# Causal attention and a gated feed-forward on one core: the last two batches' feed-forward as one product of 2 x 2 blocks

## Chip, cores, metric

One core of one Trainium2 chip runs the kernel. The metric is the device time of one execution in microseconds.

## What is computed

Four batches of 12 heads, 448 positions and 64 values a head go through causal attention; the result, 768 features for each of 1792 tokens, goes through a gated feed-forward of width 1536. All in float32.

```python
scores = scale * np.matmul(q, k.transpose(0, 1, 3, 2))
scores = np.where(mask, -1000000000.0, scores)
...
attn = attn / (np.sum(attn, axis=-1, keepdims=True) + 1e-09)
return np.matmul(attn, v).astype(np.float32)
...
gate = 1.0 / (1.0 + np.exp(-(x @ w_gate)))
val = x @ w_val
return (gate * val @ w_out).astype(np.float32)
```

## The kernel before

**Units.** The feed-forward of one batch is a unit (`unit_items`). Its first layer has 12 row blocks of the width (`KF`), each once for the gate and once for the value, with 6 K tiles (`KD`): 144 steps. The second has 6 row blocks of the output with 12 K tiles: 72 steps. A step is a triple: float32 is made of a high half (fp32r, 'xh', 'wh', 'gh') and a low one ('xl', 'wl', 'gl'), and three matmuls of 128x128 by 128x448 (L582) give high x high, high x low and low x high. One weight block serves 6 steps. Its halves are cut by ScalarE (L564) and by L566, which runs on VectorE in unit 0 and on POOL (GpSimd) afterwards. In unit 0 the weights come as int64 words, which ScalarE and VectorE (L549 to L556) turn into float32 that is also stored to DRAM ('wdram'); the later units load them from there (L561).

**First layer's end.** ScalarE takes the tanh out of PSUM (L603), VectorE multiplies (L609), ScalarE and POOL cut the product into halves (L611, L612). A unit's output leaves through ScalarE (L627).

**Attention.** Heads go in pairs, 6 pairs a batch. Batches 0 and 1 use blocks of 112 and TensorE transposes. Batches 2 and 3 (`WIDE`) use blocks of 128: scores in two bursts (L385), softmax on VectorE and ScalarE (L400, L406, L414), scaling on POOL (L421), 32x32 transposes on VectorE into 'room' (L438, L441), and then 16 transfers a pair (L447), each 32 partitions by 512 columns, which move the 32x32 blocks to the partitions where the product with V (L464, `wpv`) wants them. The product of a pair follows its last scores by two pairs. Its features are cut into halves by L351 and L352.

**Order.** Nothing is issued as it is written. Each piece is given to `Plan.op` with an engine, a cost and, for TensorE, a due time; `Plan.order` takes one piece after another, on each engine the ready one that is due first, and the program is emitted in that order. The main loop sets the due times: attention of batch 0 first, then unit `u` with the attention of batch `u + 1` spread over it; unit 3 has none beside it. Each engine runs its own list in order.

[...]

## Time and profile before

| | us |
|---|---|
| median of 3 runs | 692.42 (690.48 to 693.71) |
| the profiled execution | 692.2 |
| its span | 690.5 |
| PE busy, PEld busy | 677.6, 572.3 |
| DVE, ACT, POOL busy | 314.1, 335.3, 366.7 |
| HBM read, written | 88.08 MB, 19.66 MB |

PE is TensorE, PEld its weight loads, DVE VectorE, ACT ScalarE. Busy times of different engines overlap, so none of them is a share of the end time by itself: what an engine's time is worth shows in the stage where it runs.

### The profile page before, as it was taken

To read this page: it belongs to the slowest core of one execution; us is meant where nothing else is said; L and a number is where in the kernel's file an instruction comes from. 1 tells how busy PE (TensorE), PEld (TensorE's weight loads), DVE (VectorE), ACT (ScalarE), POOL (GpSimd) and SP (SyncE) were. 2 spreads that over 40 slices of the span, in tenths; PEclk is the share of its full clock that TensorE was granted. 3 is DMA by queue.
4 is the path that set the end of the run, shared out by engine and by line. 5 is a ranking of instruction groups with operands and counts; after the bars stand their busy time and mean duration, and the time that the engine had idled before them with its cause. 6 is when DMAs were issued, how large, how long until landed. Compare 5 with 4: busy or idle time off the path is not lost.

```text
span 690.5 us, 11031 instructions
## 1 busy us (share of the span) xinstructions
PE 677.6 (98%) x3888; PEld 572.3 (83%) x3888; DVE 314.1 (45%) x820; ACT 335.3 (49%) x721; POOL 366.7 (53%) x352
## 2 busy tenths in 40 slices
PE   7989999999999999999999999999999999999997
PEld 4546887888888888888889888888889999999997
DVE  4898998897897244353520044345440001001000
ACT  6774677667665444545532354455432333333321
POOL 3551551333631367767564467765764456666642
PEclk9999999999999999999999999999999999999999
DMA  5564686687787545545575445544645333333331
GB/s 201 188 223 158 237 304 243 204 292 252 245 298 288 169 153 155 167 142 174 162 227 176 134 133 170 174 126 140 187 140 178 124 127 115 100 106 115 116 130 41
DMA packets 45559, 121.06 MB, mean 175 GB/s; under 512 B 7104, under 2 KB 10176, under 8 KB 45504
## 3 DMA queue, kind: packets, MB, share of 16 engines
q1 hardware_dynamic: 45504, 120.35, 53.6%
q8 instruction: 31, 0.51, 0.3%
q14 instruction: 24, 0.20, 0.1%
HBM read 88.08 MB, written 19.66 MB: 156 GB/s over the span
## 4 chain that ended last, share of the span: by engine, by line
PE 94%; DVE 2%; POOL 1%; DMA 1%; ACT 1%; issue 0%; SPq 0%; ACTq 0%
PE m L582 77%; PE m L464 3%; PE s L270 3%; PE s L385 3%; PE m L343 3%; PE t L319 3%; POOL sm L306 1%; PE t L385 1%; DVE sm L283 1%; DMA room<-in_wp_dram 1%; DVE pt L330 1%; DMA raw<-in_qkt_dram 0%; ACT sm L287 0%; DVE xl L352 0%; ACT wd L549 0%
## 5 line engine op out<-in xcount | busy, mean ns | idle before, releaser
L566 POOL TENSOR_TENSOR wl<-wr,wh 128x768 fp32r<-128x768 f32 x108 | 199.1, 1843 | 167.7 <-ACT wh L564 160.8
L582 PE MATMUL m<-xh,wh 128*128 128x448 f32 x576 | 214.9, 373 | 0.0
L564 ACT CAST wh<-wr 128x768 fp32r<-128x768 f32 x144 | 120.2, 835 | 194.6 <-PE m L582 92.0
L582 PE MATMUL m<-xh,wl 128*128 128x448 f32 x576 | 210.8, 366 | 0.0
L582 PE MATMUL m<-xl,wh 128*128 128x448 f32 x576 | 210.7, 366 | 0.0
L582 PEld LDWEIGHTS m<-xh,wh 128*128 128x128 f32 x576 | 108.3, 188 | 24.0 <-issue 14.0
L582 PEld LDWEIGHTS m<-xh,wl 128*128 128x128 f32 x576 | 108.2, 188 | 8.8
L582 PEld LDWEIGHTS m<-xl,wh 128*128 128x128 f32 x576 | 108.4, 188 | 8.1
L306 POOL TENSOR_SCALAR sm<-sm,r 112x112 f32<-112x112 f32 (+1 forms) x92 | 67.8, 756 | 74.8 <-DVE r L295 56.1
L582 PE MATMUL m<-gh,wh 128*128 128x448 f32 x288 | 106.6, 370 | 0.0
L582 PE MATMUL m<-gl,wh 128*128 128x448 f32 x288 | 105.3, 366 | 0.0
L582 PE MATMUL m<-gh,wl 128*128 128x448 f32 x288 | 105.3, 366 | 0.0
L609 DVE SCALAR_TENSOR_TENSOR gt<-gt,m 128x448 f32<-128x448 f32 x48 | 29.7, 619 | 132.6 <-PE m L582 108.9
L612 POOL TENSOR_TENSOR gl<-gt,gh 128x448 fp32r<-128x448 f32 x48 | 58.2, 1212 | 48.0 <-ACT gh L611 37.2
L406 ACT ACTIVATE sm<-sm,mn 128x128 f32<-128x128 f32 (+3 forms) x84 | 43.9, 524 | 45.2 <-DVE mn L400 45.2
L582 PEld LDWEIGHTS m<-gh,wh 128*128 128x128 f32 x288 | 54.1, 188 | 6.0 <-issue 1.4
L287 ACT ACTIVATE sm<-sm,mn 112x112 f32<-112x112 f32 (+3 forms) x96 | 49.9, 521 | 18.0 <-DVE mn L283 17.7
L582 PEld LDWEIGHTS m<-gh,wl 128*128 128x128 f32 x288 | 54.1, 188 | 4.3
L582 PEld LDWEIGHTS m<-gl,wh 128*128 128x128 f32 x288 | 54.2, 188 | 4.1
L438 DVE STREAM_TRANSPOSE room<-sm 128x384 f32<-128x384 f32 (+2 forms) x84 | 35.4, 447 | 39.7 <-POOL sm L421 35.8
L400 DVE CUSTOM_DVE_ANT_0 sm<-s,mask 128x128 f32<-128x128 f32 (+1 forms) x72 | 29.3, 441 | 47.1 <-PE s L385 46.7
L421 POOL TENSOR_SCALAR sm<-sm,r 128x256 f32<-128x256 f32 (+3 forms) x84 | 41.1, 505 | 7.5 <-DVE r L416 5.7
(46 smaller groups left out, 668.8 us busy)
## 6 DMA issues: line engine op xcount, KB each, us to landing
wr<-wdram SPq DMA_DIRECT2D x108, 384.0 KB, 3.0
room<-in_wp_dram SPq DMA_DIRECT2D x36, 768.0 KB, 5.9
wdram<-wr SPq DMA_DIRECT2D x36, 384.0 KB, 5.2
pt<-room SPq DMA_DIRECT2D x192, 64.0 KB, 2.3
raw<-in_qkt_dram SPq DMA_DIRECT2D x24, 448.0 KB, 4.3
vr<-in_vt_dram SPq DMA_DIRECT2D x24, 256.0 KB, 3.5
out_dram<-gt SPq DMA_DIRECT2D x24, 224.0 KB, 2.0
```

The lines of the kernel that those rows point to most:

```text
L287: plan.op("ACT", act(ne, 0, 2), lambda z=z, sm=sm, i=i, ne=ne, off=off: nc.scalar.activation(out=sm.t[:QB, off:off + ne], in_=sm.t[:QB, of ...
L306: plan.op("PL", 0.27 + w / 1200, lambda args=args: nc.gpsimd.tensor_scalar(**args()), [(r_,)], [(sm, a)])
L385: nc.tensor.matmul(out=sp[z].t[place(z, i), o:o + ne], lhsT=r.t[h, s0:s0 + rows(i)], rhs=r.t[h, S:S + ne])
L400: plan.op("DVE", dve(ne) + 0.16, lambda z=z, y=y, sm=sm, i=i, o=o, ne=ne, off=off, s0=s0, at=at: nc.vector.tensor_tensor_reduce(out=sm.t[a ...
L406: plan.op("ACT", act(ne, 0, 2), lambda z=z, sm=sm, i=i, ne=ne, off=off: nc.scalar.activation(out=sm.t[:, off:off + ne], in_=sm.t[:, off:of ...
L421: plan.op("PL", 0.27 + w / 1200, lambda sm=sm, i=i, o=o, w=w, z=z: nc.gpsimd.tensor_scalar(out=sm.t[:, o:o + w], in0=sm.t[:, o:o + w], sca ...
L438: plan.op("DVE", dve(128 * c) + 0.1, lambda sm=sm, i=i, o=o, c=c, at=at: nc.vector.transpose(out=tv()[:, :, at:at + 32 * c].rearrange("p r ...
L564: plan.op("ACT", act(768), lambda: nc.scalar.copy(hi_.t, t.t), [(t,)], [(hi_,)])
L566: plan.op(eng, cost, lambda: at.tensor_tensor(out=lo_.t, in0=t.t, in1=hi_.t.bitcast(F32), op=ALU.subtract), [(t,), (hi_,)], [(lo_,)], lock ...
L582: nc.tensor.matmul(out=ps.t[:, :S], lhsT=a.t[:, k, :], rhs=b.t if isinstance(b, Buf) else b(), start=(first and z == 0), stop=(last and z ...
L609: plan.op("DVE", dve(S), lambda: nc.vector.scalar_tensor_tensor(out=gg.t, in0=sg.t, scalar=1.0, in1=ps.t[:, :S], op0=ALU.add, op1=ALU.mult ...
L612: plan.op("PL", 1.15, lambda: nc.gpsimd.tensor_tensor(out=gl.t[:, jj], in0=gg.t, in1=gh.t.bitcast(F32), op=ALU.subtract), [(gg,), (gh,)], ...
```

## The change

Units 2 and 3 are replaced by one pair (`pair_items`), which multiplies by Strassen's scheme in the form with seven products. The blocks: the K range in halves (`KH` = 3 tiles), the row blocks in halves, and batch 2 against batch 3. Seven half-size products, named 1 to 7, take the place of eight.

- **Inputs** (`pair_inputs`): features of batches 2 and 3 stay whole in float32 (no L352); VectorE forms the sums, and 21 tiles are cut into halves.
- **Weights** (`in_weights`, `mix`, `cut_half`): for each of 12 pairs of row blocks three loads, four sums of 384 columns on VectorE, and seven cuts of 384 columns by ScalarE and POOL. For the second layer `out_sums` forms sums once and stores them; 21 blocks are cut by ScalarE and VectorE (`cut(..., vector=True)`).
- **Products in PSUM** (`f_in`, `f_out`): 1 and 2 share a bank, 6, 7 and 4 another, 5 and 3 a third. A product adds onto what the bank holds, after VectorE (`plus`) or ScalarE (`scaled`) has read it. The order is a string, `words`: the steady word is 5, 6, 1, 7, 2, 4, 3, where 1 and 2 belong to a block three further on (`AHEAD`).
- **Second layer's inputs** (`out_inputs`): VectorE forms sums, for products 6 and 7 into PSUM ('t'), and cuts most low halves, POOL ten.
- **Attention of batch 3** moves forward: batch 1 is spread over the first 0.95 of unit 0 (`TURN`), batches 2 and 3, twelve pairs, from there to 0.85 of unit 1 (`SPREAD`). In the new order 42 matmuls of the unit (in places 39) stand between two bursts of probability times V, where 36 + 39 stood.
- **Transposed blocks** (`shift`): in place of 16 transfers one write of 1 MB to DRAM and four reads of 256 KB.
- The planner's costs of ScalarE, of the masked reduction and of a triple are changed, and with them the order everywhere.

```diff
+KH = KD // 2
...
+PAIR = 2
+TURN, SPREAD = 0.95, 0.85
+ORDER = "1256743"
+AHEAD = 3
...
-    act = lambda n, psum=0, acc=0: n / 1200 + (0.05 if psum else 0.093) + 0.093 * acc
+    act = lambda n, psum=0, acc=0: n / 1200 + (0.16 if psum else 0.19) + 0.14 * acc
...
+        if b >= PAIR:
+            x = new(f"xh{k}" if b == PAIR else f"xl{k}", [128, S], F32, 2)
+            plan.op("ACT", act(S, 1), lambda: nc.scalar.copy(x.t, vp.t[:, :S]), [(vp,)], [(x,)])
+            xs[b, k] = x
+            return
...
-        for a in range(4):
-            for r in range(4):
-                plan.op("SP", 0.64, lambda a=a, r=r: nc.sync.dma_start(
-                    out=pt.t[32 * r:32 * r + 32, a * WC:a * WC + WC], in_=tv()[32 * a:32 * a + 32, r]),
-                    [(tb, "zero", "end", *[(z, i) for z in range(2) for i in range(3)], (0, 3))], [(pt, (a, r))], extra=2.0)
+        pd = new("pd", [128, 4 * WC], F32, 2, bass.MemoryType.DRAM)
+        plan.op("SP", dma(128 * 4 * WC * 4), lambda: nc.sync.dma_start(out=pd.t, in_=tb.t),
+                [(tb, "zero", "end", *[(z, i) for z in range(2) for i in range(3)], (0, 3))], [(pd,)], extra=2.0)
+        for r in range(4):
+            plan.op("SP", dma(32 * 4 * WC * 4), lambda r=r: nc.sync.dma_start(
+                out=pt.t[32 * r:32 * r + 32, :4 * WC].rearrange("p (a n) -> p a n", a=4),
+                in_=pd.t.rearrange("(a p) (r n) -> r p a n", a=4, r=4)[r]), [(pd,)], [(pt, r)], extra=2.0)
...
+    def add(out, a, b, op, lock=True):
+        plan.op("DVE", dve(S) + 0.08, lambda: nc.vector.tensor_tensor(out=out.at, in0=a.at, in1=b.at, op=op),
+                [a.ref, b.ref], [out.ref], lock=lock)
...
+    def halves(x, hi, lo, pool=False, bank=False):
+
+        plan.op("ACT", act(S, bank), lambda: nc.scalar.copy(hi.at, x.at), [x.ref], [hi.ref])
+        if pool:
+            plan.op("PL", 1.16, lambda: nc.gpsimd.tensor_tensor(
+                out=lo.at, in0=x.at, in1=hi.at.bitcast(F32), op=ALU.subtract), [x.ref, hi.ref], [lo.ref])
+            return
+        plan.op("DVE", dve(S) + 0.08, lambda: nc.vector.tensor_tensor(
+            out=lo.at, in0=x.at, in1=hi.at.bitcast(F32), op=ALU.subtract), [x.ref, hi.ref], [lo.ref], lock=not bank)
...
+            b11, b21, b12, b22 = xa[i], xa[KH + i], xb[i], xb[KH + i]
+            for p in "56743":
+                T[p, i] = rest[p][2 * i:2 * i + 2]
+            halves(b22, *T["3", i])
+            add(b11, b12, b11, ALU.subtract)
+            add(b12, b22, b12, ALU.subtract)
+            add(b22, b22, b11, ALU.subtract)
+            add(b21, b21, b22, ALU.subtract)
+            for p, x in ("5", b11), ("6", b22), ("7", b12), ("4", b21):
+                halves(x, *T[p, i])
...
+        def take():
+
+            ring.append(part(KD * 128, len(ring) % 6))
+            return ring[-1]
...
+        def cut_half(src, at):
+
+            n = st["cuts"] = st.get("cuts", -1) + 1
+            if n % 2 == 0:
+                st["wb"] = [new(tag, [128, KD, 128], F32R, BUFS["ws"]) for tag in ("wh", "wl")]
+            (hi_, lo_), e, w = st["wb"], n % 2, KD * 64
+            f = lambda t: t.rearrange("p k m -> p (k m)")[:, e * w:e * w + w]
+            x = lambda: src.t[:, at * w:at * w + w]
+            plan.op("ACT", act(w), lambda: nc.scalar.copy(f(hi_.t), x()), [(src, at)], [(hi_, e)])
+            plan.op("PL", 1.0, lambda: nc.gpsimd.tensor_tensor(
+                out=f(lo_.t), in0=x(), in1=f(hi_.t).bitcast(F32), op=ALU.subtract), [(src, at), (hi_, e)], [(lo_, e)])
+            return (hi_, lo_), e
...
+        def in_weights(n):
+            j, gv = n // 2, n % 2
+            a = fetch(wdram[2 * j + gv])
+            c = fetch(wdram[2 * (KD + j) + gv])
+            b = take()
+            mix((b, 1, 1), (a, 0, 1), (c, 0, 1), ALU.subtract)
+            mix((c, 0, 1), (c, 0, 1), (c, 1, 1), ALU.add)
+            mix((b, 0, 1), (c, 0, 1), (a, 0, 1), ALU.subtract)
+            mix((a, 1, 1), (a, 1, 1), (b, 0, 1), ALU.subtract)
+            st["from", n] = {"5": (c, 0), "4": (c, 1), "6": (b, 0), "7": (b, 1), "3": (a, 1)}
...
+        def out_sums(m):
+
+            at = lambda mm, half: wdram[2 * KF + 2 * mm + half]
+            a11, a12, a21, a22 = (fetch(at(mm, half), new(tag, [128, KD * 128], F32, BUFS[tag]))
+                                  for mm, half, tag in ((m, 0, "wr"), (m, 1, "wr"), (KH + m, 0, "wr"), (KH + m, 1, "wd")))
+            e = lambda x: (x, 0, 2)
+            mix(e(a22), e(a21), e(a22), ALU.add)
+            mix(e(a21), e(a11), e(a21), ALU.subtract)
+            mix(e(a11), e(a22), e(a11), ALU.subtract)
+            mix(e(a12), e(a12), e(a11), ALU.subtract)
...
+        def plus(out, ps, x, scale):
+
+            b = bank(ps)
+            if scale == 1.0:
+                add(out, b, x, ALU.add, lock=False)
...
+        def f_in(n, p, k, due):
+            st["now"] = due
+            j, gv = n // 2, n % 2
+            if k == 0:
+                if p == "1":
+                    if n == 0:
+                        stage()
+                    st["raw", n] = fetch(wdram[2 * j + gv])
+                if ("from", n) not in st and p in "56":
+                    in_weights(n)
+                if p in "156":
+                    b, tag, bufs = {"1": ("x", "t", 2), "5": ("z", "s", 3), "6": ("y", "m", 3)}[p]
+                    st[b, n] = new(tag, [128, 512], F32, bufs, PSUM)
+                st["w"] = cut_half(*((st["raw", n], "12".index(p)) if p in "12" else st["from", n][p]))
+            ps = st[{"1": "x", "2": "x", "5": "z", "6": "y", "7": "y", "4": "y", "3": "z"}[p], n]
+            w, e = st["w"]
+            mm(ps, w, KH * e + k, T[p, k], p in "156" and k == 0, k == KH - 1, due, e)
...
+            def done(base, ps, sg, g):
+                g = G[g[0], j, g[1]]
+                x = bank(ps)
+                if base is not None:
+                    x = g if gv else sg
+                    plus(x, ps, base, 1.0)
+                if gv:
+                    gated(g, sg, x)
+                else:
+                    tanh(sg, x)
+
+            if p == "1":
+                scaled(p1, b, 1.0)
+            elif p == "2":
+                done(None, ps, s11, (0, 0))
+            elif p == "6":
+                plus(u2, ps, p1, 1.0)
+            elif p == "7":
+                plus(u3, ps, p1, 1.0)
+                done(u3, st["z", n], s22, (1, 1))
+            elif p == "4":
+                done(p1, ps, s21, (1, 0))
+            elif p == "3":
+                done(u2, ps, s12, (0, 1))
...
+            here = sets[e % 3]
+            for j in range(KD):
+                g11, g21, g12, g22 = G[0, j, 0], G[1, j, 0], G[0, j, 1], G[1, j, 1]
+                x = {"1": g11, "2": g21, "5": g11, "6": None, "7": None, "4": g21, "3": g22}[p]
+                if p == "5":
+                    add(g11, g12, g11, ALU.subtract)
+                if p in "67":
+                    x = bank(new("t", [128, 512], F32, 2, PSUM))
+                    add(x, g22, {"6": g11, "7": g12}[p], ALU.subtract)
+                if p == "6":
+                    add(g21, g21, x, ALU.subtract, lock=False)
+                T["o" + p, j] = here[2 * j:2 * j + 2]
+                halves(x, *T["o" + p, j], pool=p in "12543" and j % 3 == 1, bank=p in "67")
...
+        def f_out(e, m, k, due):
+            st["now"] = due
+            p = ORDER[e]
+            if m == 0 and k == 0:
+                for n in ((0, 1, 2) if e == 0 else (e + 2,)):
+                    if n < 7:
+                        out_inputs(n)
+                if p in "156":
+                    st[{"1": "x", "5": "z", "6": "y"}[p]] = [new({"1": "m", "5": "s", "6": "m"}[p], [128, 512], F32, 3, PSUM) for _ in range(3)]
+            if k == 0:
+                st["w"] = cut(fetch(sums[p, m]), vector=True)
+            ps = st[{"1": "x", "2": "x", "6": "y", "7": "y", "4": "y", "5": "z", "3": "z"}[p]][m]
+            mm(ps, st["w"], k, T["o" + p, k], p in "165" and k == 0, k == KD - 1, due)
...
+        words = ["1a1b2a2b1c5a2c"] + ["5a"[2 * (n == 0):] + "6a1d7a2d4a3a" for n in range(2 * KD - AHEAD)]
+        for n, word in enumerate(words):
+            at = max(n - 1, 0)
+            seq += [(at + "abcd".index(y), x) for x, y in zip(word[::2], word[1::2])]
+        word = "5a6a5b7a6b4a3a7b6c4b5c7c3b4c3c"
...
+    last = [PAIR * HP + k for k in range(HP)] + [(PAIR + 1) * HP + k for i in range(KH) for k in (i, KH + i)]
...
+    for seq, wide, lo, hi in ((range(HP, 2 * HP), False, 0.0, TURN), (last, True, TURN, 1 + SPREAD)):
+        steps = att_steps(seq, wide)
+        pace = [a[-1] if len(a) == 3 else a[0] for a in steps]
+        da = 0.0
+        for (c, f, *_), w in zip(steps, pace):
+            att.append((c, f, half * (lo + (hi - lo) * da / sum(pace))))
+            da += w
```

**DMA queue beside unit 1, one pair of batch 2.** Before, the 16 transfers (L447, 'pt' from 'room') stand between weight loads (L561):

```order
L561 DMA wr<-wdram_1541 128x768
L447 DMA pt<-room 32x512 x4
L561 DMA wr<-wdram_1611 128x768
L447 DMA pt<-room 32x512 x2
L561 DMA wr<-wdram_1687 128x768
L251 DMA vr<-in_vt_dram 128x512
L246 DMA raw<-in_qkt_dram 128x896
```

Now the write ('pd' from 'room') and the four reads (L456), with the next pair's loads between:

```order
L570 DMA wr<-wdram_1536 128x768
L256 DMA vr<-in_vt_dram 128x512
L251 DMA raw<-in_qkt_dram 128x896
L453 DMA pd<-room 128x2048
L570 DMA wr<-wdram_1573 128x768
L456 DMA pt<-pd 32x4x512 x4
```

The reads stand behind the loads of the next pair, and wait for the write; the weight loads behind them wait too.

**VectorE beside the last units.** Before, the list ends with the last softmax and transposes, the low halves of the last features, and then nothing but the gating of unit 3:

```order
L414 TENSOR_SCALAR r<-sum 128x1
L416 RECIPROCAL r<-r 128x1
L438 STREAM_TRANSPOSE room<-sm 128x3x4x32
L441 STREAM_TRANSPOSE room<-sm 128x2x32
L352 TENSOR_TENSOR xl_5657<-m,xh_5651 128x448
L352 TENSOR_TENSOR xl_5805<-m,xh_5800 128x448
L609 SCALAR_TENSOR_TENSOR gt<-gt,m 128x448 x12
```

Now, in one word of the pair's first layer ('m', 's', 't' are PSUM banks, 'xh' and 'xl' here hold partial results, 'room' weights): the read of product 6, four weight sums for the next block, the read of product 7 and its sum with 5, a gating, the reads of products 4 and 3:

```order
L672 TENSOR_TENSOR xl0_4982<-m_5427,xh0_4862 128x448
L766 TENSOR_TENSOR room_418<-room_418 128x384 x4
L672 TENSOR_TENSOR xl2_5019<-m_5427,xh0_4862 128x448
L672 TENSOR_TENSOR xl3_5029<-s_5410,xl2_5019 128x448
L826 SCALAR_TENSOR_TENSOR gh3_5490<-xh5_4968,t_5439 128x448
L672 TENSOR_TENSOR xl4_5054<-m_5427,xh0_4862 128x448
L672 TENSOR_TENSOR xl5_5075<-s_5410,xl0_4982 128x448
```

The four weight sums stand ahead of the read of product 7.

**VectorE in the second layer of the pair**, where before it had no instruction: the inputs of product 6, with the low halves of a later weight block (L744) between them:

```order
L744 TENSOR_TENSOR wl_6433<-room_418,wh_6427 128x768
L672 TENSOR_TENSOR t_6441<-gl_5149,gh4_5700 128x448
L672 TENSOR_TENSOR t_6448<-gl_5149,gh5_6111 128x448
L672 TENSOR_TENSOR gh10_6069<-gh10_6069,t_6441 128x448
L682 TENSOR_TENSOR xl4_5915<-t_6441,xh4_5908 128x448
L672 TENSOR_TENSOR gh11_6182<-gh11_6182,t_6448 128x448
L744 TENSOR_TENSOR wl_6470<-room_418,wh_6460 128x768
```

'gl' less 'gh' goes into PSUM ('t'), is taken off 'gh' and cut.

## Rows read from the trace of the kernel before

**Rows 1.** Busy time of each engine (us, in brackets the instructions) by stage

```profile
core 0: us, PE busy (x) PEld busy (x) DVE busy (x) ACT busy (x) POOL busy (x), PEclk, DMA share, GB/s
0.00:62.40 62.40, 53.16 (x324) 30.26 (x324) 48.58 (x163) 41.49 (x125) 27.18 (x52) 0.97 0.55 191
62.40:234.60 172.20, 172.20 (x950) 143.43 (x949) 144.99 (x250) 108.86 (x220) 63.05 (x64) 1.00 0.74 256
234.60:395.00 160.40, 160.40 (x986) 138.53 (x985) 56.51 (x198) 70.55 (x157) 100.32 (x96) 1.00 0.54 164
395.00:555.30 160.30, 160.30 (x985) 138.43 (x984) 56.60 (x198) 70.55 (x156) 100.09 (x94) 1.00 0.50 152
555.30:690.50 135.20, 131.51 (x649) 121.63 (x648) 7.46 (x12) 43.85 (x65) 76.09 (x46) 1.00 0.32 106
```

**Rows 2.** Chain of waits, 280 to 310 us and its last long piece: start, us, what

```profile
283.53 1.93 PE m L464 x40
285.46 0.90 PE s L385 x4
286.36 7.50 PE m L582 x36
293.85 0.86 PE s L385 x8
294.71 0.64 PE t L385 x4
295.35 8.11 PE m L582 x39
303.46 1.93 PE m L464 x40
305.38 0.90 PE s L385 x4
...
545.56 141.27 PE m L582 x696
```

**Rows 3.** Timeline of the end: start us, us, engine, line, operation [idle before]

```profile
686.44 0.37 PE L582 MATMUL m<-gh,wl 128*128 128x448 f32 x1
686.85 0.54 ACT L627 ACTIVATE gt<-m 128x448 f32<-128x448 f32 x1 [5.54 <-PE m L582]
687.42 0.33 SPq L629 DMA_DIRECT2D out_dram<-gt  x1
```

**Rows 4.** Groups of equal instructions: busy us, mean ns | idle before, releaser

```profile
L566 POOL TENSOR_TENSOR wl<-wr,wh 128x768 fp32r<-128x768 f32 x108 | 199.1, 1843 | 167.7 <-ACT wh L564 160.8 <-DMA pt<-room 3.9 <-DMA wr<-wdram 1.9
L564 ACT CAST wh<-wr 128x768 fp32r<-128x768 f32 x144 | 120.2, 835 | 194.6 <-PE m L582 92.0 <-POOL wl L566 40.3 <-issue 28.1
...
L566 DVE TENSOR_TENSOR wl<-wr,wh 128x768 fp32r<-128x768 f32 x36 | 34.7, 965 | 9.1 <-ACT wh L564 9.1
...
L609 DVE SCALAR_TENSOR_TENSOR gt<-gt,m 128x448 f32<-128x448 f32 x48 | 29.7, 619 | 132.6 <-PE m L582 108.9 <-issue 16.5 <-ACT sm L406 7.2
L611 ACT CAST gh<-gt 128x448 fp32r<-128x448 f32 x48 | 27.1, 565 | 3.5 <-DVE gt L609 1.9
L603 ACT ACTIVATE gt<-m 128x448 f32<-128x448 f32 x48 | 25.9, 539 | 18.5 <-PE m L582 18.3
```

**Rows 5.** Timeline of VectorE behind the scores of one pair, 306 to 320 us

```profile
306.31 0.62 DVE L400 CUSTOM_DVE_ANT_0 sm<-s,mask 64x448 f32<-64x448 f32 x1
...
315.24 0.58 DVE L438 STREAM_TRANSPOSE room<-sm 128x384 f32<-128x384 f32 x1 [4.87 <-POOL sm L421]
...
319.54 0.24 DVE L441 STREAM_TRANSPOSE room<-sm 128x64 f32<-128x64 f32 x1
```

**Rows 6.** DMA issues: line, count, KB each, median us from issue to landing

```profile
wr<-wdram SPq DMA_DIRECT2D x108, 384.0 KB, 3.0
room<-in_wp_dram SPq DMA_DIRECT2D x36, 768.0 KB, 5.9
...
pt<-room SPq DMA_DIRECT2D x192, 64.0 KB, 2.3
raw<-in_qkt_dram SPq DMA_DIRECT2D x24, 448.0 KB, 4.3
vr<-in_vt_dram SPq DMA_DIRECT2D x24, 256.0 KB, 3.5
```

**Rows 7.** Timeline of the DMA queue: issues of one pair's transposed blocks

```profile
305.23 5.57 SPq L447 DMA_DIRECT2D pt<-room  x9
```

**Rows 8.** Timeline, VectorE and POOL at the same time, 158 to 164 us

```profile
157.96 1.15 POOL L612 TENSOR_TENSOR gl<-gt,gh 128x448 fp32r<-128x448 f32 x1
...
157.99 1.94 DVE L556 SCALAR_TENSOR_TENSOR wr<-wd,wr 128x768 int32<-128x768 int32 x1
...
163.53 0.96 DVE L556 SCALAR_TENSOR_TENSOR wr<-wd,wr 128x768 int32<-128x768 int32 x1
```

221 lines of the change are left out of this document (185 added, 36 removed).

## Prediction

> **What bounds the kernel now.** I read the stage table first, then the chain of waits, then the last microseconds. [rows 1] cut the span where the matmuls of each unit (one batch's feed-forward) begin. [...] [rows 2] show what one costs: 696 matmuls in a row take 141.27 us, 0.203 us each, so a triple (three matmuls on one K tile) takes 0.609 us. The same rows give the bursts of one head pair between them: 1.93 + 0.90 + 0.86 + 0.64 = 4.33 us. [rows 3] show the end: last matmul at 686.44, ScalarE's emptying of 0.54 us, one transfer, end at 690.5. The profiled execution took 692.2 us, 1.7 more than its span, and stands 0.2 below the median of 692.42.
>
> **Removed: matmuls.** Units 2 and 3 have 2 x 216 = 432 triples. The pair has 12 x 7 x 3 = 252 in its first layer and 7 x 3 x 6 = 126 in its second, 378 in all. That is 54 triples or 162 matmuls fewer: 162 x 0.203 = **32.9 us**, all on the path, since TensorE has no idle time in these stages. 692.2 - 32.9 = **659.3 us** if nothing else waits.
>
> **Moved: attention of batch 3.** Six pairs go from beside unit 2 to beside unit 1. TensorE's work stays the same in sum (6 x 4.33 = 26 us change stage; unit 1's grows to about 186 us). The other engines there, from [rows 1]: a pair's share of VectorE is (56.5 - 12 x 0.62 - 6 x 0.62) / 6 = 7.6 us with [rows 4] for the gating and the low halves, so 56.5 + 6 x 7.6 - 3.7, and 33 operations of 0.62 for the pair's inputs, make 119 us of 186. In the same way (stage less 36 casts, 12 low halves and so on of the unit itself) six pairs cost ScalarE 27 us and POOL 20: 110 with the 21 casts of the pair's inputs, and 121. Nobody is full, so I cost the load at nothing.
>
> What shrinks is the time a pair has. Between two probability-times-V bursts stood 36 + 39 matmuls [rows 2], and in the new order 42 (in places 39); so one period is 42 x 0.203 + 4.33 = 12.9 us, and from the end of the last scores to the burst that needs the transposed result lie two periods less the 2.83 us of that step: 22.9 us. In that time go softmax, 32x32 transposes, and now a round trip through DRAM. In the trace a pair's scores end at 306.28 [rows 2] and its last transpose at 319.8 [rows 5]: 13.5 us, with 5 us of VectorE idle in it; in the new order I take 10 us. The round trip is one write of 1 MB and four reads of 256 KB, which no row has. [rows 6] give two slopes: from 64 KB (2.3 us) to 384 KB (3.0 us) 2.2 us a MB, from vr's 256 KB (3.5) to raw's 448 KB (4.3) 4.2 us a MB. The write takes 4.4 us by the first from 384 KB, and 7.2 us from the 768 KB row at 5.9 us; the reads 5.2 to 7.3 us (one at 3.5 us, 768 KB more behind it). So 9.6 to 14.5 us; I take 12, which is what it replaces: nine of sixteen issues took 5.57 us [rows 7], so all 16 take 9.9 us, and the last needs 2.3 us to land. 10 + 12 = 22 of 22.9 us: no wait, but with no room. The low end leaves 3 us; the high end, with 13.5 us ahead of it, makes 28, and then the period is (28 + 2.83) / 2 = 15.4 us, 2.5 us late for each of 11 pairs.
>
> [...]
>
> **Added: the pair's first layer**, 252 triples, 153.5 us, in words of seven products (12.8 us). VectorE: 84 sums and gatings of 448 columns at 0.62 us, 48 weight sums of 384 at 0.55 (between 0.619 for 448 and 0.965 for 768, [rows 4]) and 12 of 768: 52 + 26 + 12 = 90 us. ScalarE: 84 casts of 384 at 0.51 (from 0.565 and 0.835) and 36 of 0.54: 62 us. POOL: 84 low halves at about 1.0 us (half of 1.843; its 448 columns took 1.15 in [rows 8]): 85 us. All lie beside TensorE's 153.5. What can show is a handover. Product 7 adds onto the bank of product 6, and product 4 onto that of 7, after VectorE has read it; one other product, 1.83 us, lies between. VectorE's read takes 0.62 and must not stand behind anything longer than 1.1 us. In each word four weight sums stand ahead of the read of 7. They wait for the place that product 3 of the word before leaves, whose cut starts when product 6 ends: 0.51 + 1.0 + 0.3 for the handoffs = 1.8 us, then 4 x 0.55 = 2.2, so the read starts 4.0 us after product 6, ends at 4.7, and product 4 is due at 3 x 1.83 = 5.5. That holds; each cut of POOL that comes between adds 1.0.
>
> Whether it does: [rows 8] show a VectorE operation on two SBUF operands (L556) started 0.03 us behind one of POOL's, 1.94 us long instead of 0.96: it waited until POOL's 1.15 us were over. One such wait gives 5.7 against 5.5, 0.2 to 0.3 late; two give 1.3. For 11 words: 0 to 14 us. I take one, **3 us**.
>
> [...]
>
> **The second layer**, 126 triples, 76.7 us: VectorE has 71 operations of 0.62 and 21 low halves of 0.965, 44 + 20 = 64 us, and up to 11.5 us more if it waits for each of POOL's ten. It is nearly full, but prepares a product's inputs while two others run (11 us each): 0 to 5 us, I take 0. The tail gets 0.1 us. **The head** has new costs in its planner and so another order; it may win or lose a third of its 9.2 us of idle time: 0, between -3 and +3.
>
> Sum: 692.2 - 32.9 + 3 = **662 us**; the forecast's own bounds are 655 (head) and 670.
>
> **Rivals.**
> (a) *The round trip comes late.* For it: 22 of 22.9 us and a high end of 28. Against it: the low end, and VectorE only 64% full. It costs 0.5 to 2.5 us for each of 11 pairs; with 1.5 us, 662 + 16 = 678 us.
> (b) *VectorE bounds the second layer.* For it: 64 + 11.5 of 76.7 us, in one queue with cuts that wait for TensorE. If a product's inputs come late and two more handovers with them, some 8 us: 670.
> (c) *VectorE and POOL alternate in the pair's first layer*, the slower case. If each of the six operations on two SBUF operands in a word (four weight sums, two gatings) waits for one whole cut, VectorE has 7.5 + 6.1 = 13.6 us in a 12.8 us word with the bank reads behind them, and TensorE pays that and its handovers, 16 us a word: 11 x 3.2 = 35 us, 694.5. It decides from 3.3 us a word ((692.2 + 3.5 - 659.3) / 11). For it: the 1.94 us row. Against: POOL is busy 7.1 us of a word, so half the operations meet none, and unit 0's stage held TensorE at 100% with VectorE at 84%.
>
> **How the numbers follow.** Forecast 0.62, (a) 0.16, (b) 0.14, (c) 0.05, and 0.03 for waits of several kinds that eat the gain without passing it. The range 655 to 680 takes in the forecast's bounds, (b), and (a) up to its middle. A measurement here tells 0.5%, 3.5 us, from no change. Faster: 0.62 + 0.16 + 0.14 = 0.92; same 0.03; slower 0.05.
>
> **What would show it.** Right: 1134 matmuls of the pair in some 231 to 236 us at clock 1.00, unit 1's stage near 186 us, and small waits of product 4 for VectorE's sums. (a) shows as TensorE waiting for DMA at the probability-times-V bursts, (b) as waits of the second layer for VectorE's halves, (c) as weight sums of 1.5 us and more and a pair stage over 260 us. The forecast is wrong if the pair takes over 240 us, or the stage of unit 1 over 192.

## The result, and the profile after

The changed kernel takes 667.13 us (median of 4 runs, 666.39 to 670.97) against 692.87 us before: a ratio of 0.9645, 95% interval 0.9601 to 0.9690. Five more runs of it beside other kernels gave 668.90 us and 0.9656 (0.9631 to 0.9681). The forecast was 662 us, faster; the sign and the mechanism came as said, the gain is 25.7 us of the 30 forecast.

The profiled execution took 667.55 us with a span of 665.8, against 692.2 and 690.5 before. The stages, as in [rows 1], cut at the first matmul of a unit (63.65, the end of the head), of the pair (428.93) and of its second layer (584.27):

```profile
core 0: us, PE busy (x) PEld busy (x) DVE busy (x) ACT busy (x) POOL busy (x), PEclk, DMA share, GB/s
0.00:63.65 63.65, 53.96 (x325) 30.70 (x325) 49.25 (x164) 41.59 (x126) 26.32 (x52) 0.95 0.55 187
63.65:428.93 365.28, 361.42 (x2271) 298.48 (x2270) 278.83 (x659) 214.82 (x488) 189.87 (x208) 1.00 0.79 258
428.93:584.27 155.34, 155.34 (x757) 141.96 (x756) 99.53 (x144) 63.73 (x129) 94.36 (x84) 1.00 0.44 145
584.27:665.80 81.53, 78.00 (x379) 70.75 (x377) 61.23 (x90) 33.65 (x57) 8.19 (x6) 1.00 0.30 101
```

TensorE is busy for all of the pair; the only idle time between the head and the last matmul is in the second row, 365.28 - 361.42 = 3.86 us. The table of TensorE's waits (engine, line, releaser: us, times, longest) names the places (0.3 us more are for a weight half at L591):

```profile
PE m L473 <- DMA pt<-pd: 2.1, 2, 1.7
...
PE m L473 <- DVE mn L410: 1.4, 1, 1.4
```

L473 is the product with V of the wide pairs. It waited at the first pair (258.5 us), the seventh (339.4) and the twelfth (401.1), 1.5, 0.5 and 1.8 us. The table puts the first down to VectorE (L410), but the last of that pair's four reads landed at 259.90 us and the product began at 260.25, so the round trip held it as well until then. In the pair (L803) no wait is listed. The chain of waits there (start, us, what):

```profile
429.09 9.12 PE t L803 x45
...
443.74 1.86 PE t L803 x9
...
585.06 20.96 PE m L803 x102
```

The first five products have the period of the units, 9.12 / 45 = 0.2027 us a matmul. After them it is more: 1.86 / 9 = 0.2067, 20.96 / 102 = 0.2055. The 1134 matmuls last from 428.93 to 662.1, 233.2 us, 0.2056 each, where [rows 2] have 0.2030.

So the spans compare like this, by stages and terms:

| term | forecast, us | measured, us |
|---|---|---|
| 162 matmuls fewer | -32.9 | -32.9 |
| handovers of the first layer | +3 (0 to 14) | 0 |
| round trip through DRAM (0.3 of it the weight half) | 0 (0 to 28) | +3.9 |
| second layer, VectorE | 0 (0 to 5) | 0 |
| head | 0 (-3 to 3) | +1.2 |
| tail | +0.1 | -0.2 |
| period of a matmul in the pair | not named | +2.9 (1134 x 0.0026) |
| sum | -29.8 | -25.1; span -24.7 |

The forecast came as near as it did in part by luck: 3 us too much for the handovers hide part of the 8 us that the round trip, the period and the head cost and that it had at nothing.

### The profile page after: what moved, and what is told of

Its sections match the earlier page's. It is cut to its first block, busy times and chain, and to the rows that moved or that the text cites. A ratio compares the mean times of both kernels' runs of the same rounds, so it can differ in the third digit from the quotient of the medians.

```text
span 665.8 us, 10888 instructions
## 1 busy us (share of the span) xinstructions
PE 648.7 (97%) x3726; PEld 541.9 (81%) x3726; DVE 488.8 (73%) x1053; ACT 353.8 (53%) x799; POOL 318.7 (48%) x350
## 4 chain that ended last, share of the span: by engine, by line
PE 87%; DVE 5%; DMA 4%; POOL 1%; issue 1%; ACT 1%; SPq 0%; ACTq 0%
PE m L591 36%; PE m L803 18%; PE s L803 10%; PE t L803 7%; PE m L348 3%; PE s L275 3%; PE m L473 3%; PE s L395 3%; PE t L324 3%; DMA pt<-pd 2%; DMA pd<-room 2%; DVE sm L288 1%; POOL sm L311 1%; PE t L395 1%; DVE pt L335 1%
## 5 line engine op out<-in xcount | busy, mean ns | idle before, releaser
L757 POOL TENSOR_TENSOR wl<-room,wh 128x384 fp32r<-128x384 f32 x84 | 93.6, 1137 | 56.7 <-ACT wh L756 54.6
L591 PE MATMUL m<-xh,wh 128*128 128x448 f32 x288 | 109.3, 380 | 0.0
L591 PE MATMUL m<-xh,wl 128*128 128x448 f32 x288 | 105.3, 366 | 0.3 <-DVE wl L575 0.3
L591 PE MATMUL m<-xl,wh 128*128 128x448 f32 x288 | 105.3, 365 | 0.0
L575 POOL TENSOR_TENSOR wl<-wr,wh 128x768 fp32r<-128x768 f32 x36 | 67.6, 1879 | 57.8 <-ACT wh L573 57.8
L573 ACT CAST wh<-wr 128x768 fp32r<-128x768 f32 x72 | 59.8, 832 | 41.9 <-DVE wr L565 20.3
L591 PEld LDWEIGHTS m<-xh,wh 128*128 128x128 f32 x288 | 54.1, 188 | 19.5 <-issue 12.0
L292 ACT ACTIVATE sm<-sm,mn 112x112 f32<-112x112 f32 (+2 forms) x96 | 50.0, 522 | 21.2 <-DVE mn L288 20.2
L591 PEld LDWEIGHTS m<-xh,wl 128*128 128x128 f32 x288 | 54.1, 188 | 5.1 <-DVE wl L575 0.7
L591 PEld LDWEIGHTS m<-xl,wh 128*128 128x128 f32 x288 | 54.2, 188 | 3.8
L591 PE MATMUL m<-gh,wh 128*128 128x448 f32 x144 | 53.9, 374 | 0.0
L591 PE MATMUL m<-gh,wl 128*128 128x448 f32 x144 | 52.6, 366 | 0.0
L591 PE MATMUL m<-gl,wh 128*128 128x448 f32 x144 | 52.6, 365 | 0.0
L410 DVE CUSTOM_DVE_ANT_0 sm<-s,mask 128x128 f32<-128x128 f32 (+1 forms) x72 | 29.6, 439 | 23.0 <-PE s L395 22.6
L803 PE MATMUL m<-pt,wh 128*128 128x448 f32 x150 | 45.0, 368 | 0.0
L431 POOL TENSOR_SCALAR sm<-sm,r 128x384 f32<-128x384 f32 (+3 forms) x84 | 41.1, 510 | 8.1 <-DVE r L426 8.1
L575 DVE TENSOR_TENSOR wl<-wr,wh 128x768 fp32r<-128x768 f32 x36 | 35.6, 990 | 12.0 <-ACT wh L573 12.0
```

The costliest lines, as they stand in the source:

```text
L292: plan.op("ACT", act(ne, 0, 2), lambda z=z, sm=sm, i=i, ne=ne, off=off: nc.scalar.activation(out=sm.t[:QB, off:off + ne], in_=sm.t[:QB, of ...
L431: plan.op("PL", 0.27 + w / 1200, lambda sm=sm, i=i, o=o, w=w, z=z: nc.gpsimd.tensor_scalar(out=sm.t[:, o:o + w], in0=sm.t[:, o:o + w], sca ...
L573: plan.op("ACT", act(768), lambda: nc.scalar.copy(hi_.t, t.t), [(t,)], [(hi_,)])
L575: plan.op(eng, cost, lambda: at.tensor_tensor(out=lo_.t, in0=t.t, in1=hi_.t.bitcast(F32), op=ALU.subtract), [(t,), (hi_,)], [(lo_,)], lock ...
L591: nc.tensor.matmul(out=ps.t[:, :S], lhsT=a.t[:, k, :], rhs=b.t if isinstance(b, Buf) else b(), start=(first and z == 0), stop=(last and z ...
L757: plan.op("PL", 1.0, lambda: nc.gpsimd.tensor_tensor(out=f(lo_.t), in0=x(), in1=f(hi_.t).bitcast(F32), op=ALU.subtract), [(src, at), (hi_, ...
```

## Experiments

Each is the changed kernel with the edit shown. "Units" is the time from the first matmul of a unit to the first of the pair, 365.28 us in the changed kernel.

### The transposed blocks in 16 transfers again

```diff
-        pd = new("pd", [128, 4 * WC], F32, 2, bass.MemoryType.DRAM)
...
+        for a in range(4):
+            for r in range(4):
+                plan.op("SP", 0.64, lambda a=a, r=r: nc.sync.dma_start(
+                    out=pt.t[32 * r:32 * r + 32, a * WC:a * WC + WC], in_=tv()[32 * a:32 * a + 32, r]),
...
```

> The changed kernel (667.1 us) with one part undone: the transposed blocks of a pair of heads go in 16 transfers of 64 KB again instead of one write and four reads. The prediction priced both ways alike, 12 us from the first issue to the last landing; by that the time stays at 667 within 2 us. Rival: the queue of SP is the limit. 16 issues of 0.62 us are 9.9 us, and with two inputs of 0.38 and some six weight loads and stores of 0.33 about 12.7 us of a period of 12.9 to 13.2 us; weight loads and the next pair's inputs would come late, TensorE would wait in the stage of unit 1, and the time would be 672 to 690 us.

681.56 us, ratio 0.9834 (0.9810 to 0.9859). The units take 380.40 us, 15 more; the pair is as before (155.8 + 77.8). The rival holds. TensorE's wait at the product with V, and the queue of SP beside one pair of heads (start, us, issues):

```profile
PE m L471 <- DMA pt<-room: 10.3, 4, 3.5
```

```profile
337.15 6.22 SPq L454 DMA_DIRECT2D pt<-room  x10
...
345.54 3.68 SPq L454 DMA_DIRECT2D pt<-room  x6
```

Before the change the same issues had a period of 19.9 us (283.53 to 303.46 in [rows 2]). Here the queue has no free time: ten issues, four loads and six issues follow one another from 337.15 to 349.2 us, 12 us of a period of 13. The prediction had priced the two ways alike, by the latency of one pair. Measured, the 16 transfers are even the quicker way, 11.4 to 14.5 us from first issue to last landing over the twelve pairs against 12.7 to 15.9; what differs is the queue's load. The write with four reads is the part of the change without which some 14 of its 26 us would be lost.

Only part of the 15 us in the units is waiting. Their row, and that of the longest of three stretches (13.6 us together) in which the clock fell to 0.50 at such a wait:

```profile
63.00:443.40 380.40, 367.39 (x2270) 302.84 (x2269) 273.25 (x653) 212.88 (x485) 192.26 (x208) 0.98 0.67 215
```

```profile
375.21:382.03 6.82, 5.64 (x45) 4.16 (x46) 0.24 (x1) 2.20 (x3) 4.12 (x6) 0.50 0.75 231
```

TensorE's idle time is 380.40 - 367.39 = 13.0 us against 3.9, 9.2 more; its busy time is 6.0 us longer than the 361.42 of the changed kernel, with the same matmuls.

What the round trip loads instead is seen in two rows of the stage table over the stretch 280 to 395 us, ahead of the change and with it:

```profile
280.00:395.00 115.00, 115.00 (x755) 100.58 (x754) 36.67 (x121) 45.85 (x96) 70.74 (x67) 1.00 0.55 170
```

```profile
280.00:395.00 115.00, 114.59 (x858) 93.45 (x857) 76.87 (x261) 65.15 (x170) 77.59 (x94) 1.00 0.91 286
```

The DMA engines go from 0.55 to 0.91 busy, 170 to 286 GB/s. With 16 transfers the stretch has 0.62 and 184 GB/s, so most of the rise is the round trip's own. The transfers of that stretch that both kernels have are longer with the change. The DMA issues in it (count, KB each, median us to landing), ahead of the change and with it:

```profile
wr<-wdram SPq DMA_DIRECT2D x26, 384.0 KB, 3.3
...
raw<-in_qkt_dram SPq DMA_DIRECT2D x4, 448.0 KB, 4.9
vr<-in_vt_dram SPq DMA_DIRECT2D x6, 256.0 KB, 3.5
```

```profile
pd<-room SPq DMA_DIRECT2D x9, 1024.0 KB, 6.4
pt<-pd SPq DMA_DIRECT2D x32, 256.0 KB, 5.3
wr<-wdram SPq DMA_DIRECT2D x21, 384.0 KB, 6.1
raw<-in_qkt_dram SPq DMA_DIRECT2D x5, 448.0 KB, 7.6
vr<-in_vt_dram SPq DMA_DIRECT2D x8, 256.0 KB, 6.4
```

And the seventh pair's trip in the chain of waits, which ends with the wait of 0.5 us:

```profile
324.58 5.83 DMA pd<-room
331.74 8.20 DMA pt<-pd
340.18 2.00 PE m L473 x40
```

From the write's issue to the last landing are 331.74 + 8.20 - 324.58 = 15.4 us.

### Another pace for the wide pairs: longer, later, and with true latencies

Three edits of the plan for the 3.9 us:

```diff
-TURN, SPREAD = 0.95, 0.85
+TURN, SPREAD = 0.95, 0.92
```

> The changed kernel with the twelve wide pairs spread to 0.92 of unit 1 instead of 0.85, so that a period is some 0.7 us longer and from a pair's scores to its product there are some 1.5 us more. Theory: the 3.9 us that TensorE waits at L473 in three places (1.5, 0.5 and 1.8 us) are a round trip that is late by those amounts; two of them go or shrink, and the time falls by 2 to 4 us, to 663 to 665. Rival: the lateness only moves to the pair's inputs, whose last sums and cuts end at 427 us now and would end some 12 us later, behind the start of product 5 at 438; the time stays at 667 or rises to 672.

```diff
-TURN, SPREAD = 0.95, 0.85
+TURN, SPREAD = 0.92, 0.85
...
-                        L.append((0, lambda due: None, 1.0))
+                        L.append((0, lambda due: None, 1.5))
```

> The changed kernel with the wide pairs started at 0.92 of unit 0 instead of 0.95 and the two last steps of the attention, which have no scores, spread 1.5 times as far. In the changed kernel the product of the last pair was planned 20.4 us after its scores, where the others had 22.5 to 24.5, and TensorE waited 1.8 us for it; the first wide pair waited 1.5 us and the seventh 0.5. Theory: it is the time between scores and product that is short in these places; with 22 us or more for all, the three waits go and the time falls by 3 to 4 us, to 663 to 664. Rival: the waits come from the queue of SP, where a write or read stands behind a weight load that waits for its place; they come back at other pairs and the time is 666 to 670.

```diff
-                [(tb, "zero", ...)], [(pd,)], extra=2.0)
+                [(tb, "zero", ...)], [(pd,)], extra=4.6)
...
-                in_=...[r]), [(pd,)], [(pt, r)], extra=2.0)
+                in_=...[r]), [(pd,)], [(pt, r)], extra=5.0)
```

> The changed kernel with the planner told what the round trip takes: the latency of the write (its 'extra') 4.6 instead of 2.0 us, that of the four reads 5.0 instead of 2.0. In the changed kernel the queue of SP stood 26 us in eight places at a read that waited for the write, with weight loads and inputs behind it; now weight loads and inputs are put ahead of the reads, and the write is due earlier. Theory: the three waits of 3.9 us at the product with V are this planning; they shrink to 2 us or less, and the time falls by 2 to 4 us (663 to 665). Rival: the round trip has no more time than before whatever stands around it, and loads ahead of the reads make it later: the waits stay or grow, 667 to 672.

And the changed kernel once more, beside the last:

> The changed kernel as it is, for the comparison with the two runs before on one chip: 667 us by its four runs so far (666.4 to 671.0). If its head and its waits at the product with V vary from run to run, the profile shows other ones than 63.65 us and 1.5, 0.5 and 1.8 us, while the pair stays at 233.2 us.

| kernel | us | ratio (95%) | units, us | TensorE idle in them | at half the clock | waits at L473: first, seventh, last pair |
|---|---|---|---|---|---|---|
| spread 0.92 | 672.80 | 0.9716 (0.9690 to 0.9741) | 369.97 | 5.5 | 6.8 | 0, 0, 4.8; 0.6 at the eleventh |
| last steps 1.5 times as far | 671.05 | 0.9684 (0.9657 to 0.9711) | 366.16 | 3.7 | 0 | 0.4, 0, 2.3; 0.4 at the fourth |
| latencies 4.6 and 5.0 | 674.50 | 0.9740 (0.9716 to 0.9763) | 372.06 | 8.0 | 6.8 | 2.0, 1.1, 4.9 |
| the change again | 668.90 | 0.9656 (0.9631 to 0.9681) | 366.63 | 3.9 | 3.4 | 1.4, 0, 2.3 |

The changed kernel's first profile has 365.28, 3.9 and 0 in these columns. None of the three is faster, so the theory fails in each; the times lie 0.8 to 2.5 us above what the rivals said. Part of the longer units with a spread of 0.92 and with the true latencies is the clock: 3.1 and 2.7 us of it are longer busy time, with 6.8 us at clock 0.50 behind the last pair's wait.

With a spread of 0.92 the first and the seventh wait are gone, as the theory has it: their products began 22.9 and 24.9 us behind the scores. But the last pair's transposes ended 10.4 us behind its scores instead of 7.0. Its scaling on POOL (L431) stood behind a weight half (L575), and VectorE worked on the pair's inputs between the transposes (L445); the write followed at once:

```profile
393.53 1.85 POOL L575 TENSOR_TENSOR wl<-wr,wh 128x768 fp32r<-128x768 f32 x1 [1.14 <-ACT wh L573]
395.36 2.87 POOL L431 TENSOR_SCALAR sm<-sm,r 128x256 f32<-128x256 f32 x4
```

```profile
398.00 0.58 DVE L445 STREAM_TRANSPOSE room<-sm 128x128 f32<-128x128 f32 x2
```

```profile
398.60 0.32 SPq L453 DMA_DIRECT2D pd<-room  x1
```

With the last steps stretched the last pair's product stood 24.9 us behind its scores, but its transposes took 13.7 us, between the same kinds of other work, and the wait is there again. Its write, too, followed the last transpose at once, so the queue of that run's rival was not what held it. With true latencies the time that SP's queue stands at a read waiting for its write falls from 38.1 us in 12 places to 7.2 in 5 (the 26 us of the expectation are those of the run with spread 0.92), and TensorE waits more, not less: the loads that went ahead of the reads make the reads late (6.8 and 6.7 us to landing for write and reads, against 6.1 and 5.8), and a trip takes 14.6 to 18.2 us instead of 12.7 to 15.9. So the three waits are not one cause that a planner's number removes. That the load of the DMA engines is what makes the trips long is argued from the rows of the section before, not tried by itself.

### The planner's costs and the head

Former costs everywhere:

```diff
-    act = lambda n, psum=0, acc=0: n / 1200 + (0.16 if psum else 0.19) + 0.14 * acc
+    act = lambda n, psum=0, acc=0: n / 1200 + (0.05 if psum else 0.093) + 0.093 * acc
...
-                plan.op("DVE", dve(ne) + 0.16, lambda z=z, sm=sm, i=i, o=o, ...
+                plan.op("DVE", dve(ne) + 0.08, lambda z=z, sm=sm, i=i, o=o, ...
...
-    qk_cost = lambda blocks: sum((i + 1) * QB / 600 + 0.14 for i in blocks) + 0.1
+    qk_cost = lambda blocks: sum((i + 1) * QB / 600 + 0.18 for i in blocks) + 0.2
```

> The changed kernel with the planner's former costs of ScalarE, of the masked reduction and of narrow scores. Theory: the 1.2 us that the head is longer (63.65 against 62.43 us to the first matmul of a unit) come from these costs alone, so the head is 62.4 us again; the time falls by 1 us, if the wide pairs' stage stays as it is. Rival: the costs serve the wide pairs, whose softmax is then planned too early or late, and the waits at L473 grow by more than the head gains: 668 to 675 us.

667.81 us, 0.9637 (0.9616 to 0.9659): the same as the change. The head is 61.61 us, the units 368.24: what one wins the other gives back, as waits at L473 (2.2 and 3.4 us) and 3.4 us at half the clock behind the second.

And, with the latencies of the run above, in the attention of batch 0 alone:

```diff
+    head = [True]
+    act = lambda n, psum=0, acc=0: n / 1200 + ((0.05 if psum else 0.093) + 0.093 * acc if head[0] else (0.16 if psum else 0.19) + 0.14 * acc)
...
+                plan.op("DVE", dve(ne) + (0.08 if head[0] else 0.16), lambda z=z, sm=sm, i=i, o=o, ...
...
     now -= 3.0
+    head[0] = False
```

> As the run before, and the attention of batch 0 alone planned by the former costs of ScalarE, the masked reduction and narrow scores. With those costs everywhere the head was 61.6 us and not 63.65, but the waits of the wide pairs grew by 3 us. Theory: the two are apart, so the head is 61.5 to 62.5 us and the rest as in the run before: 1 to 2 us less than that run. Rival: the head's length varies by as much from run to run (62.96 to 64.46 so far with the new costs), or the units start on another foot and give it back: no difference.

671.50 us, 0.9698 (0.9675 to 0.9721), with a head of 66.11 us: the theory of the head fails, the same costs give 61.6 in one run and 66.1 in the other. The time is 3.0 us less than that of the run with the latencies, but through the units: 367.50 us, with 2.6 us less idle time and 3.4 us less at half the clock. The granted clock shows why the heads differ. In the head TensorE idles 0.5 to 0.9 us at a time, and behind some of that idle time the granted clock goes from 1.00 to 0.50, for 3.4 to 10.2 us of a head. Two rows of the stage table, cut where the clock falls and rises, before the change and with it:

```profile
54.63:58.04 3.41, 3.41 (x18) 1.74 (x15) 2.16 (x11) 1.23 (x5) 0.00 (x0) 0.50 0.01 4
```

```profile
52.44:59.26 6.82, 6.33 (x28) 3.74 (x28) 4.99 (x14) 1.43 (x6) 1.14 (x1) 0.50 0.34 115
```

3.41 us at half the clock in the one, 6.82 in the other; in the head of 61.6 us it was 3.41, in that of 66.1 us 10.2. Ahead of the fall stand four idle gaps of 0.5 to 0.8 us from 47.1 us on with the change, two of 0.6 and 0.9 us from 51.6 us on before it. Three other runs with the new costs in the head had 3.41 us at half the clock and heads of 62.96 to 63.35 us; seven had 6.83 us, as the change itself, and 63.56 to 64.77. So of the +1.2 us only some 0.5 are one more such stretch, which comes or not from run to run; with a single stretch the head is still 0.5 to 0.9 us longer than in the one profile before the change, and that goes with the new order.

### Four more weight sums a word

```diff
-            mix((b, 1, 1), (a, 0, 1), (c, 0, 1), ALU.subtract)
+            for _ in range(5):
+                mix((b, 1, 1), (a, 0, 1), (c, 0, 1), ALU.subtract)
```

> The changed kernel with four more weight sums of 384 columns in each word of the pair's first layer (the first sum is written five times; the result is the same). VectorE's work in a word of 12.9 us goes from 7.5 to 9.7 us without waits. Theory: reads of a bank start 0.04 us behind a product and the next product on that bank comes 1.04 us after the read, so a sum ahead of a read costs nothing while it is shorter than that: 667 us, at most 670. Rival (VectorE and POOL alternate): each extra sum waits for a whole cut of POOL of 1.0 us, 4 x 1.6 = 6.4 us more a word, 14 us of 12.9, and the time rises by 1 to 2 us for each of 11 words or more: 680 to 690 us.

683.52 us, 0.9887 (0.9849 to 0.9924). The pair's first layer takes 169.23 us instead of 155.35, the rest as before: the rival's size. Of these 13.9 us 7.3 are idle time of TensorE (155.34 busy of 155.34 us became 161.94 of 169.23) and 6.6 longer busy time, in which 6.8 us at clock 0.50 behind two of the waits take part. But the rival's mechanism is smaller than it said: 22 of the 96 sums lasted over 0.7 us, and a sum more cost VectorE (70.7 - 32.8) / 48 = 0.79 us and not 1.6. Nor is it the only one. ScalarE's casts now wait for the sums (groups: busy us, mean ns | idle before, releaser):

```profile
L766 DVE TENSOR_TENSOR room<-room 128x384 f32<-128x384 f32 x96 | 70.7, 740 | 6.8 <-POOL wl L757 4.7
L756 ACT CAST wh<-room 128x384 fp32r<-128x384 f32 x84 | 38.9, 511 | 69.0 <-DVE room L766 34.7 <-POOL wl L757 11.9 <-PE s L804 9.8
```

A sum takes 0.740 us on average, a little more than in the changed kernel (0.689, below); but 34.7 us of ScalarE's idle time ends with a sum, a releaser that its row of the changed kernel does not name. The chain load, eight sums, cast, cut, product became longer. To tell the two apart, the extra instructions took one operand from a PSUM bank:

```diff
-            mix((b, 1, 1), (a, 0, 1), (c, 0, 1), ALU.subtract)
+            ps, w = st["x", min(n + 2, 2 * KD - 1)], KD * 64
+            for _ in range(4):
+                plan.op("DVE", 0.1 + w / 960, lambda: nc.vector.tensor_tensor(
+                    out=b.t[:, w:2 * w], in0=ps.t[:, :w], in1=a.t[:, :w], op=ALU.subtract), [(ps,), (a, 0)], [(b, 1)])
+            mix((b, 1, 1), (a, 0, 1), (c, 0, 1), ALU.subtract)
```

> As the run with four more weight sums a word (683.5 us), but the four extra instructions take one operand from a PSUM bank instead of SBUF; their place in VectorE's list, their 384 columns, their target and the sums behind them are as there (they are written over by the right sum). Theory: that run lost 13.9 us in the pair's first layer because sums with two SBUF operands and POOL's cuts stop each other; with a PSUM operand they pass, and the first layer is back at 155.4 us to 159, the time at 667 to 671. Rival: the loss was VectorE's queue and the longer chain from loads to the cuts by themselves; the first layer stays at 166 us or more, the time at 679 to 684.

696.12 us, 1.0019 (0.9991 to 1.0046), the whole gain lost; the first layer takes 182.72 us. The rows:

```profile
L756 ACT CAST wh<-room 128x384 fp32r<-128x384 f32 x84 | 39.2, 511 | 71.9 <-DVE room L766 54.1 <-PE s L807 7.0 <-PE m L591 6.1
L766 DVE TENSOR_TENSOR room<-room 128x384 f32<-128x384 f32 x48 | 33.0, 691 | 0.9
L776 DVE TENSOR_TENSOR room<-t,room 128x384 f32<-128x384 f32 x48 | 26.7, 555 | 22.0 <-ACT xh L826 8.2 <-ACT xh L834 4.8 <-PE t L807 4.3
```

The edit brought a wait of its own: L776 stood 22 us for the bank that it reads, with the sums behind it, and ScalarE waited 54.1 us for those. So it does not decide how much of the 13.9 us is the mutual stop and how much the chain; that stays open. What it does show: 48 instructions with a PSUM operand lasted 0.555 us on average, none over 0.56, though seven of them ran beside a cut of POOL for over 0.3 us; the sums with two SBUF operands among them had 0.691, the 15 longest 0.75 to 1.36, each of them beside a cut. In these rows a cut of POOL holds up a sum of two SBUF operands, and an instruction with one operand in PSUM keeps its 0.555 us.

### The period of a matmul

```diff
         if tag not in pools:
+            if tag in ('vr',):
+                gap = "gap_" + tag
+                pools[gap] = ctx.enter_context(tc.tile_pool(name=gap, bufs=1))
+                pools[gap].tile([128, 8], F32, tag=gap, name=gap)
```

> The changed kernel, its instructions the same, with 32 unused bytes in each partition of SBUF ahead of the tile 'vr', so that every operand of the feed-forward's matmuls begins at a multiple of 64 bytes. In the changed kernel the tiles 'raw' and 'sm' begin at such a multiple, and all others (features, 'pt', weights) 32 bytes behind one. TensorE's period in the pair was 0.2056 us a matmul, where a unit without attention had 0.2027; the first five products, which read 'xh' and 'xl' alone, had 0.2027, and the first product that reads 'raw' was followed by 0.2061 to 0.2067. Theory: the mixture of the two offsets sets off the longer period; with one offset for all it is 0.2027 throughout, the pair takes 2.9 to 3.3 us less, and the time is 663 to 665. Rival: the offset has no part in it (the banks, the order of products or the data have); the pair stays at 233 us and the time at 667.

```diff
-            if tag in ('vr',):
+            if tag in ('raw', 'vr'):
```

> As the run before, with 32 unused bytes ahead of 'raw' too, so that every operand begins 32 bytes behind a multiple of 64, as in the units of the kernel before. Theory of the mixture: 0.2027 us a matmul in the pair, 663 to 665 us, as with the other common offset. Second theory: the offset of 0 is the slow one by itself; then this run is fast (0.2027) and the other is at 0.2061 or more. Rival: neither moves, 667 us.

670.77 us, 0.9682 (0.9657 to 0.9707), and 668.88 us, 0.9648 (0.9624 to 0.9671): neither apart from the change. The pair is 231.9 and 232.0 us instead of 233.2, 0.2045 us a matmul, in both alike. So something about where the operands lie takes part (without a wait in the pair no other run was under 233.2), but it does not explain the longer period. The trace has no addresses, so that the offsets are equal is not shown by itself. In every steady word of the changed kernel the seven products, from product 1 on, take 0.2061, 0.2067, 0.2067, 0.2064, 0.2059, 0.2038 and 0.2044 us a matmul; in these two runs 0.2063, 0.2067, 0.2067, 0.2059, 0.2030, 0.2018 and 0.2022. Product 1 keeps the longer period in both. The first rows of the pair in the one run and in the other:

```profile
432.19 9.12 PE t L807 x45
```

```profile
431.84 9.30 PE t L807 x45
```

The same five products take 9.12 in one and 9.30 us in the other. And in the run with 16 transfers a wait inside the pair changed the period of the products behind it, with the operands that they always have:

```profile
471.69 0.85 issue
...
475.35 1.82 PE t L801 x9
...
499.15 1.86 PE m L801 x9
```

Behind the wait two words ran at 0.2022 to 0.2037 us, and then the longer periods were back without another wait. So the same products take between 0.202 and 0.207 us a matmul at the same granted clock of 1.00. What sets it stays open.

### The second layer without POOL

```diff
-                halves(x, *T["o" + p, j], pool=p in "12543" and j % 3 == 1, bank=p in "67")
+                halves(x, *T["o" + p, j], pool=False, bank=p in "67")
```

> The changed kernel with the ten low halves of the second layer that POOL cuts given to VectorE. VectorE was busy 61.0 us of 77.8 there, 4.5 us of it in five instructions that lasted 1.5 us instead of 0.62; it gets ten more of 0.62, 6.2 us, and loses the long ones: some 63 us. Theory: VectorE has room, the second layer stays at 77.8 us without a wait, and the time is 667. Rival (VectorE bounds the second layer): each of the ten stands in one queue with cuts that wait for TensorE, inputs come late by 0.6 to 1.2 us for each of five products, and the time is 670 to 673 us.

668.74 us, 0.9674 (0.9636 to 0.9713). The second layer takes 77.83 us, as in the changed kernel, without a wait. VectorE does not bound it, with POOL's help (61.23 us busy of 81.53) or without (59.39 of 81.54).

## Why the prediction was right, and where it was off

**The matmuls.** Right: 54 triples fewer, none replaced by waits in the pair. The rows above have TensorE busy for 155.34 of 155.34 us. The unit 1 stage, 239.6 to 428.93, took 189.3 us against "near 186", inside the bound of 192; six pairs cost 160.3 - 131.5 = 28.8 us of TensorE's time by [rows 1] and not the 26 us of bursts alone, which changes only this check.

**The handovers: 3 us forecast, 0 measured.** The step that failed is "They wait for the place that product 3 of the word before leaves, whose cut starts when product 6 ends", and on it "I take one" wait for POOL a word. VectorE in the trace (start, us, idle before):

```profile
482.66 0.62 DVE L672 TENSOR_TENSOR xl<-m,xh 128x448 f32<-128x448 f32 x1 [3.05 <-PE m L803]
483.28 2.34 DVE L766 TENSOR_TENSOR room<-room 128x384 f32<-128x384 f32 x4
486.37 0.62 DVE L672 TENSOR_TENSOR xl<-m,xh 128x448 f32<-128x448 f32 x1 [0.76 <-PE m L803]
...
497.09 2.33 DVE L766 TENSOR_TENSOR room<-room 128x384 f32<-128x384 f32 x4 [0.85 <-POOL wl L757]
499.34 0.62 DVE L672 TENSOR_TENSOR xl<-m,xh 128x448 f32<-128x448 f32 x1
```

In the first word shown the sums start right behind the read of product 6, their place long free, and end 0.76 us before the read of 7 is due; in the second they wait 0.85 us for a cut and end as it falls due. In all nine steady words the read of 7 starts 0.04 to 0.05 us behind its product, and product 4 begins 1.0 us after the read has ended. The sums start 0.6 or 1.5 us behind product 6 in these words and not 1.8; the 0.3 us for the handoffs in that was the author's estimate, which no row shows, and in the second word cast, cut and first sum follow one another with 0.08 and 0.03 us between them. A cut that holds them up is absorbed.

**VectorE and POOL** do stop each other, as [rows 8] made one expect, but the sums less often than the forecast's one wait a word; in the changed kernel's groups:

```profile
L757 POOL TENSOR_TENSOR wl<-room,wh 128x384 fp32r<-128x384 f32 x84 | 93.6, 1137 | 56.7 <-ACT wh L756 54.6 <-DMA room<-wdram 1.3 <-DMA sum<-wd 0.8
...
L766 DVE TENSOR_TENSOR room<-room 128x384 f32<-128x384 f32 x48 | 32.8, 689 | 4.1 <-POOL wl L757 3.2
...
L672 DVE TENSOR_TENSOR xl<-m,xh 128x448 f32<-128x448 f32 x30 | 18.7, 623 | 33.2 <-PE m L803 33.0
```

The sums take 0.689 us on average instead of 0.55 and the cuts 1.14 instead of 1.0, the reads of a bank 0.623 as ever. Of the 84 cuts 62 lasted 1.01 to 1.07 us and 22 lasted 1.33 to 1.74, each of these 22 beside a VectorE instruction with two SBUF operands; the 30 reads of a bank had 0.61 to 0.63, though 18 of them ran beside a cut for over 0.5 us. Only 8 of the 48 sums, four a word, lasted over 0.7 us (0.78 to 2.21), each beside a cut; the others had 0.55 to 0.62. Rival (c) did not come: the first layer has VectorE at 99.5 of 155.3 us. The runs with extra sums put the edge between four and eight sums a word.

**The round trip: 0 forecast, 3.9 us measured, rival (a) in its smallest form.** Of "22 of 22.9 us: no wait, but with no room" the 22 were near, as the sum of two terms that were off. The trip itself was mis-sized: 12 us with a high end of 14.5 in the forecast, 12.7 to 15.9 us over the twelve pairs, 14.6 on average. Its price was read from rows at a DMA share of 0.50 to 0.54 [rows 1, 6], and the new stage runs at 0.91. The part ahead of the write took 4.5 to 8.5 us, 6.4 on average, and not 10. Together that is 17.7 to 23.9 us.

The step that failed is the 22.9 us, one period for all: "from the end of the last scores to the burst that needs the transposed result lie two periods less the 2.83 us of that step". It holds for ten of the pairs, whose products began 22.6 to 24.6 us behind their scores, waits left out. The first pair had 21.2 us and the last 18.8, since the last two steps hold no scores (the "20.4" of the expectations has the wait in it). The chain of waits has the scores and the product of both, and the last pair's trip:

```profile
236.84 0.90 PE s L395 x4
...
260.25 2.00 PE m L473 x40
...
381.86 0.90 PE s L395 x4
...
389.77 5.30 DMA pd<-room
396.41 6.64 DMA pt<-pd
403.19 2.00 PE m L473 x40
```

The first pair needed 22.2 us and the last 20.4: with the same needs both would have been in time at 22.9 us. Only the seventh was late from the common place, by the longest sum of all, 8.5 + 15.4 = 23.9 us of 23.7.

The four reads took 7.2 to 10.1 us over the twelve pairs from first issue to last landing, 9.5 in the seventh pair; what of that is due to the load of the DMA engines no run here tells.

**The second layer** is as forecast: 77.8 us and no wait, with VectorE at 61 us against 64 forecast. Rival (b) is ruled out by the run without POOL.

**The head** cost 1.2 us, inside its bounds of 3, in part through the granted clock and not through the planner's order alone.

**What the prediction did not name** is the period of a matmul in the pair, 2.9 us. It took 0.203 us from 696 matmuls in a row [rows 2] for a stream with other operands.
